# One step of attention in a slot, and weight norms taken from squares on ScalarE

## The chip, the core and the metric

The kernel runs on one core of a Trainium2 chip. TensorE (PE in the profile) multiplies, VectorE (DVE), ScalarE (ACT) and GpSimd (POOL) work on tiles, and SyncE (SP) starts most of the transfers. PSUM is the memory that TensorE writes its products into: here eight banks of 128 x 512 float32, three under the tag `acc` and five under the tag `w`. The metric is the device time of one launch in microseconds (us).

## What is computed

Attention with a window of 32 keys (in heads 4 to 7 every fourth key of the last 128), then a gated layer, then a second layer, on 4 x 576 = 2304 tokens of width 512:

```python
scores = scale * np.matmul(q, k.transpose(0, 1, 3, 2))        # 4 x 8 heads, 576 x 576, width 64
scores = np.where(masks[None, :, :, :], scores, -1000000000.0)
attn = softmax(scores)                                         # exp(s - max) / (sum + 1e-9)
x = (attn @ v), as 2304 x 512

xn = x / sqrt(mean(x * x) + 1e-6) * rms_g                      # the norm
g = xn @ w_gate;  val = xn @ w_val                             # 512 x 1536 each
y = (g * sigmoid(g) * val) @ w_out                             # 1536 x 512

h = y @ w_in                                                   # 512 x 2048
out = (max(h, 0) + alpha * min(h, 0)) @ w_out2                 # 2048 x 512
```

## The kernel before

**Products in three passes.** Each large operand is split into two float16 halves, high and low, and a product is three matmuls: high by high, high by low, low by high. Before it is split, a weight is scaled by a power of two. The scale of w_gate, w_val and w_out comes from a bound on the norms of their columns. The weights arrive as packed integers: `decode_w` turns them into float32 with three VectorE instructions for a block, or for a pair of blocks (lines 227, 228, 229). `norm_w` is called for each block after its decoding. For the 36 blocks of the first layer it forms, in bfloat16, the product of the block with itself on TensorE (`gram`, four 128 x 128 matmuls a block) and takes the row maximum on VectorE (line 281), up to four blocks to a reduction. The 12 columns of blocks come in two chunks, of 3 and of 9. When a chunk's last w_val block is in, `gram_w1` sends the maximum over the partitions (`over_partitions`, lines 335 and 338) through `root_scale` (lines 343 to 346); only then does `split_w` (lines 407 to 412) split that chunk's weights and the matmuls of `mm1` use them.

**Tokens and slots.** The tokens lie in seven blocks j of 256, 256, 384, 384, 384, 256 and 384 columns. Phase A of a block is the gated layer (`mm1`, 24 matmuls of a slot, then `mm2`, which sums into the `acc` tiles), phase B the second layer (`mm3`, 12 matmuls of a slot, then `mm4`). The order is A0, A1, A2, B0, B1, B2, A3, the first four slots of A4, B3, the rest of A4, A5, A6; the second layer of the last three blocks follows as a tail with fewer products (`mm3_t`, `mm4_t`, `out_t`), from about 813 us on. Each phase has 12 (A) or 16 (B) slots, one for each block of 128 columns of the layer's width.

**Attention between the slots.** Attention is cut into 52 groups of up to 128 queries. Groups 0 to 18 work in float32 (`f_` functions); the 33 groups from 19 on in float16 halves. Such a group takes two steps, and each step does one part of several groups at once: `first_half(i)` splits q and k of group i-1 into the tile `qkhl` (lines 538 to 552), computes the scores and softmax of group i-2 (`a_score`; it ends with `phl`, the probabilities in two halves, whose low half POOL makes on line 704), and issues two transposing transfers on SP: `qkT<-qkhl` (line 562) and `pT<-phl` (line 710). `second_half(i)` does the products with v of group i-3, the squares of group i and the next loads. A group's norm is a third kind of step. `qkhl` and `qkT` have one buffer each, so the scores of successive groups pass through one chain: split on ACT and DVE, transfer, eight score matmuls `psw<-qkT`, next split.

**What sets the order.** A planner at build time calls `take(d)` before each slot. It adds to a credit what the due times of the remaining steps ask for in that slot's time, and hands out steps, one for each unit of credit, up to two a slot. The steps run under a raised priority, and a scheduler then puts each engine's instructions into one fixed order. The weights are decoded by `pump`, called in the early slots.

Of the kernel before, what the change touches and what calls it, by code (L numbers as in the profile page):

```python
# [29 lines left out]
def kernel(  # L30
# [14 lines left out]
    nc = tc.nc  # L45
# [57 lines left out]
    def b_v(c):  # L103
        return 3 * c + 1

    def b_o(c):
        return 3 * c + 2
# [127 lines left out]
        d = dec_at[b]  # L235
        return wb[:, d * 512:(d + 1) * 512]

    def head(b):
        d = dec_at[b]
        return wbb[:, d * 1024:(d + 1) * 1024].rearrange("p (k f t) -> p k f t", f=128, t=2)[:, :, :, 1]  # L240

    def half(b, l):
        d = hl_at[b]
        return wb16[:, d * 1024 + l * 512:d * 1024 + (l + 1) * 512]
# [19 lines left out]
        ch = chunk(b // 3)  # L264
        return 2 * NCH + ch if b % 3 == 2 else 2 * ch + b % 3

    nrm = const.tile([128, 2, 3], F32, name="nrm")
    sqo = const.tile([128, NCH], F32, name="sqo")

    def gram(blocks, sums, dst):  # L270

        g = psw()
        last = len(blocks) - 1
        for n, b in enumerate(blocks):
            for kc in range(KD):
                w = head(b)[:, kc, :]
                if sums:
                    mm(g[:, 0:128], w, w, n + kc == 0, n == last and kc == KD - 1)
                else:
                    mm(g[:, n * 128:(n + 1) * 128], w, w, kc == 0, kc == KD - 1)  # L280
        nc.vector.tensor_reduce(dst, g[:, 0:128 if sums else (last + 1) * 128], axis=AX.X, op=ALU.max)

    def gram_w1(ch):
        cs = list(range(ch0[ch], ch0[ch + 1]))
        if len(cs) == 2:
            g = psw()
            for n, b in enumerate([f(c) for f in (b_g, b_v) for c in cs]):
                for kc in range(KD):
                    w = head(b)[:, kc, :]
                    mm(g[:, n * 128:(n + 1) * 128], w, w, kc == 0, kc == KD - 1)  # L290
            nc.vector.tensor_reduce(nrm[:, :, 0], g.rearrange("p (a c) -> p a c", a=2), axis=AX.X, op=ALU.max)
            parts = 1
        else:
            parts = (len(cs) + 3) // 4
            for a, f in enumerate((b_g, b_v)):
                for n in range(parts):
                    gram([f(c) for c in cs[4 * n:4 * n + 4]], False, nrm[:, a, n:n + 1])
        t = nrm[:, :, 0]
        if parts > 1:
            nc.vector.tensor_reduce(tmp2, nrm[:, :, 0:parts], axis=AX.X, op=ALU.max)  # L300
            t = tmp2
        over_partitions(t, 2, wp_[:, 0:2])
        two = slice(2 * ch, 2 * ch + 2)
        root_scale(wp_[:, 0:2], wsg[:, two], wrc[:, two])
        nc.vector.tensor_scalar(tsc[:, ch:ch + 1], xsc[:, 1:2], wrc[:, 2 * ch:2 * ch + 1], 0.5, ALU.mult, ALU.mult)

    def norm_w(b):
        if b < NW1:
            ch = chunk(b // 3)
            if b % 3 < 2:  # L310
                if b == b_v(ch0[ch + 1] - 1):
                    gram_w1(ch)
            elif b == b_o(ch0[ch + 1] - 1):
                gram([b_o(c) for c in range(ch0[ch], ch0[ch + 1])], True, sqo[:, ch:ch + 1])
        else:

            n, p = (b - NW1) // 2, (b - NW1) % 2
            junk = wk.tile([128, 512], BF16, tag="junk", bufs=1, name="junk")
            nc.scalar.activation(junk, dec(b), ACTF.Square, accum_out=sq2[:, p, n:n + 1])
            if b == NBLK - 1:  # L320
                g = psw()
                sb = const.tile([128, 2], F32, name="sb")
                nc.vector.tensor_reduce(sb, sq2, axis=AX.X, op=ALU.add)
                mm(g[:, 0:2], ones_1, eps[:, 0:2], True, False)
                mm(g[:, 0:2], ones_1, sb.bitcast(BF16).rearrange("p (n t) -> p n t", t=2)[:, :, 1], False, True)
                nc.vector.tensor_copy(sb2, g[:, 0:2])
# [791 lines left out]
    def out_t(t):  # L1118
# [50 lines left out]
    def take(d):  # L1169

        rate = max([(n - state["done"]) / max(when - state["clock"], 1.0) for n, when in need] + [0.0])
        state["credit"] = min(state["credit"] + rate * d, 4.0)
        got = []
        while steps and state["credit"] >= 1.0 and len(got) < 2:
            j = steps[0][1]
            if j is not None and j >= NXY and j - NXY not in done_b:
                break
            got.append(steps.popleft()[0])
            state["done"] += 1
            state["credit"] -= 1.0  # L1180
        return got
# [180 lines left out]
```

## Time and profile before

| | us |
|---|---|
| median of 3 runs (lowest, highest) | 984.36 (982.41, 986.07) |
| the profiled execution | 981.89 |
| its span | 980.0 |
| PE busy | 919.9 (94%) |
| DVE busy | 649.1 (66%) |
| ACT busy | 577.2 (59%) |
| POOL busy | 320.9 (33%) |
| SP's and other hardware queues' packets, share of 16 engines | 36.1% |
| granted TensorE clock, mean | 0.975 |

The span is what the profiler saw of the program, and the execution's time is 1.89 us longer. PE is busy for 94% of the span, so a change shows in the time mostly by what it does to the other 6%, to stretches in which PE's clock is lower, and to the first eighth of the span, where PE is not the busiest engine. "Idle before" in the rows below is the time in which an engine did nothing just before an instruction, with the engine and line whose result it then got.

### The profile page before, as it was taken

How to read it: one execution, taken by the hardware profiler on the slowest of the kernel's cores; microseconds unless marked ns; L12 is line 12 of the kernel's file. 1: busy time of each engine (PE TensorE's matmuls, PEld its weight loads, DVE VectorE, ACT ScalarE, POOL GpSimd, SP SyncE). 2: the span in 40 equal slices, each digit the busy share in tenths (PEclk: the TensorE clock that was granted, in tenths of full speed). 3: DMA queues.
4: the chain of work that ended last, by engine and by line, in shares of the span. 5: the costliest groups of instructions: out<-in, count | busy, mean ns of one | idle time of the engine just before them, and what ended most of it. 6: DMA issues, size and time to landing. Idle time of an engine off the chain costs nothing.

```text
span 980.0 us, 19290 instructions
## 1 busy us (share of the span) xinstructions
PE 919.9 (94%) x6958; PEld 628.0 (64%) x6958; DVE 649.1 (66%) x1586; ACT 577.2 (59%) x1600; POOL 320.9 (33%) x326
## 2 busy tenths in 40 slices
PE   5477899999999999999999989999999999999997
PEld 3466766775556666545555645555676557889986
DVE  4999997898898555554455565434454836776675
ACT  3434687676899876676655687644534325454553
POOL 2111631131354743332422233422352612332331
PEclk9777999999999999999999999999999999999999
DMA  9993436455445263452534564231311001000000
GB/s 254 315 354 98 116 99 187 119 182 147 91 85 96 58 121 65 92 103 61 117 64 83 98 111 87 53 82 29 52 27 22 1 1 33 1 23 2 23 23 22
DMA packets 191614, 88.15 MB, mean 90 GB/s; under 512 B 176800, under 2 KB 180384, under 8 KB 191520
## 3 DMA queue, kind: packets, MB, share of 16 engines
q1 hardware_dynamic: 189504, 83.27, 36.1%
q10 hardware_dynamic: 2016, 3.67, 1.1%
q8 instruction: 54, 0.88, 0.4%
q14 instruction: 40, 0.33, 0.1%
HBM read 55.32 MB, written 6.55 MB: 63 GB/s over the span
## 4 chain that ended last, share of the span: by engine, by line
PE 58%; DVE 3%; DMA 3%; ACT 2%; issue 2%; POOL 1%; SPq 0%; DVEq 0%; ACTq 0%; POOLq 0%
PE psw L95 25%; PE acc L95 17%; PE p L95 16%; DMA qkT<-qkhl 1%; DMA rkv<-in_k_dram 1%; DMA pT<-phl 1%; DVE wb L1049 0%; ACT wb L1048 0%; DMA xyall<-yhl 0%; ACT junk L512 0%; ACT s L589 0%; ACT qkhl L538 0%; ACT wb L407 0%; DVE s L1042 0%; DMA scratch<-xd 0%
## 5 line engine op out<-in xcount | busy, mean ns | idle before, releaser
L95 PEld LDWEIGHTS <-wb 128*128 128x128 f16 (+1 forms) x4917 | 458.3, 99 | 203.6 <-issue 11.8
L95 PE MATMUL psw<-xyall,wb 128*128 128x384 f16 (+1 forms) x2784 | 431.4, 304 | 2.7 <-DVE t L920 1.4
L95 PE MATMUL acc<-wb,hlall 128*128 128x512 f16 x771 | 187.7, 380 | 1.1 <-ACT hlall L923 0.6
L95 PEld LDWEIGHTS <-hlall 128*128 128x128 f16 x771 | 74.2, 98 | 74.5 <-ACT hlall L923 1.4
L929 POOL TENSOR_TENSOR hlall<-t,hlall 128x384 f16<-128x384 f32 (+1 forms) x56 | 53.8, 960 | 151.3 <-ACT hlall L923 126.8
L95 PE MATMUL acc<-wb 128*128 128x512 f16 x357 | 87.9, 384 | 3.2 <-ACT wb L987 1.9
L95 PE MATMUL p<-xyall,wb 128*128 128x256 f16 (+1 forms) x960 | 88.6, 251 | 0.0
L1097 POOL TENSOR_TENSOR wb<-fa,wb 128x640 f16<-128x640 f32 x32 | 47.0, 1472 | 108.5 <-ACT wb L1096 99.2
L95 PE MATMUL p<-wb 128*128 128x256 f16 x672 | 77.4, 273 | 0.0
L919 ACT ACTIVATE t<-psw,tsc 128x384 f32<-128x384 f32 (+1 forms) x84 | 44.2, 526 | 50.7 <-PE psw L95 50.5
L920 DVE SCALAR_TENSOR_TENSOR t<-t,psw 128x384 f32<-128x384 f32 (+1 forms) x84 | 41.0, 488 | 42.2 <-ACT t L919 42.0
L985 DVE SCALAR_TENSOR_TENSOR p<-m,nal,p 128x256 f32<-128x256 f32 (+1 forms) x64 | 42.9, 670 | 38.9 <-ACT p L984 37.8
L407 ACT ACTIVATE wb<-wb,wsg 128x512 f16<-128x512 f32 x68 | 46.0, 715 | 22.6 <-DVE wsg L345 15.6
L95 PE MATMUL psw<-wb 128*128 128x128 bf16 (+6 forms) x448 | 52.4, 284 | 6.4 <-DVE wb L229 6.4
L704 POOL TENSOR_TENSOR phl<-s,phl 96x512 f16<-96x512 f32 (+2 forms) x33 | 36.0, 1090 | 66.2 <-ACT phl L698 41.3
L589 ACT ACTIVATE s<-s,mx 96x128 f32<-96x128 f32 (+2 forms) x132 | 50.1, 384 | 11.4 <-DVE mx L581 11.3
L929 POOL TENSOR_TENSOR wb<-t,wb 128x256 f16<-128x256 f32 (+1 forms) x28 | 25.5, 911 | 95.3 <-ACT wb L923 84.0
L929 POOL TENSOR_TENSOR hlall<-p,hlall 128x256 f16<-128x256 f32 (+1 forms) x45 | 37.3, 829 | 51.9 <-ACT hlall L987 40.8
L921 DVE SCALAR_TENSOR_TENSOR t<-t,psw 128x384 f32<-128x384 f32 (+1 forms) x84 | 41.1, 490 | 18.4 <-PE psw L95 17.1
L1096 ACT ACTIVATE wb<-fa 128x640 f16<-128x640 f32 x32 | 23.6, 737 | 50.1 <-DVE fa L1089 50.1
L1095 DVE SCALAR_TENSOR_TENSOR wb<-fa,wb 128x384 f16<-128x384 f32 x32 | 40.9, 1286 | 18.0 <-ACT wb L1094 17.5
L410 POOL TENSOR_TENSOR wb<-wb 128x512 f16<-128x512 f32 x28 | 38.9, 1392 | 40.5 <-DVE wb L412 18.9
(197 smaller groups left out, 1403.2 us busy)
## 6 DMA issues: line engine op xcount, KB each, us to landing
wb<-in_moe_w_out_dram SPq DMA_DIRECT2D x28, 512.0 KB, 4.4
wb<-in_moe_w_in_dram SPq DMA_DIRECT2D x16, 512.0 KB, 3.8
wb<-in_moe_w_gate_dram SPq DMA_DIRECT2D x12, 512.0 KB, 7.0
wb<-in_moe_w_val_dram SPq DMA_DIRECT2D x12, 512.0 KB, 7.0
out_dram<-o ACTq DMA_DIRECT2D x14, 256.0 KB, 2.6
rkv<-in_k_dram SPq DMA_DIRECT2D x23, 128.0 KB, 2.7
rkv<-in_v_dram SPq DMA_DIRECT2D x23, 128.0 KB, 2.9
rq<-in_q_dram SPq DMA_DIRECT2D x23, 96.0 KB, 2.0
```

The source lines that it names most:

```text
L95: nc.tensor.matmul(o, a, b, start=start, stop=stop)
L407: nc.scalar.activation(half(b, 0), dec(b), ACTF.Copy, scale=wsg[:, s:s + 1])
L410: nc.gpsimd.tensor_tensor(half(b, 1), dec(b), half(b, 0), ALU.subtract)
L589: nc.scalar.activation(s[:nq, h, :nk], s[:nq, h, :nk], ACTF.Exp, bias=mx[:nq, 1, h:h + 1], accum_out=g["dn"][:nq, h])
L704: nc.gpsimd.tensor_tensor(phl[:nq, 1, :, :nk], g["s"][:nq, :, :nk], phl[:nq, 0, :, :nk], ALU.subtract)
L919: nc.scalar.activation(t[:, :T], pg[:, :T], ACTF.Tanh, scale=tsc[:, chunk(c):chunk(c) + 1])
L920: nc.vector.scalar_tensor_tensor(t[:, :T], t[:, :T], 1.0, pg[:, :T], ALU.add, ALU.mult)
L921: nc.vector.scalar_tensor_tensor(t[:, :T], t[:, :T], 2.0 ** -46, pv[:, :T], ALU.mult, ALU.mult)
L929: nc.gpsimd.tensor_tensor(a[:, 1, :T], t[:, :T], a[:, 0, :T], ALU.subtract)
L985: nc.vector.scalar_tensor_tensor(p[:, :T], m[:, :T], nal[:, c:c + 1], p[:, :T], ALU.mult, ALU.add)
L1095: nc.vector.scalar_tensor_tensor(l[:, 0:3], f[:, 0:3], 0.25, h[:, 0:3], ALU.mult, ALU.subtract)
L1097: nc.gpsimd.tensor_tensor(l[:, 3:8], f[:, 3:8], h[:, 3:8], ALU.subtract)
```

## The change

Three edits:

- **Norms.** `gram` and `gram_w1` go. `columns(b)` squares a block on ScalarE into one of four bfloat16 buffers (they lie in the third of the tiles that later hold the tokens' halves, `xyall`), and four matmuls, with 128 x 128 of the squares as the weights and one column of ones as the moving operand, write the column sums into a tile `cols` of PSUM, one column for each block. `cols` takes one of the three `acc` banks while the norms are formed. VectorE then reduces `cols` once a chunk (new line 289), and twice a chunk for w_out (new lines 296 and 297).
- **Last scaling.** For the last tile of the tail, the second half is scaled on VectorE in place, and its transfer starts from ACT's queue; the first half stays on ScalarE (line 1002).
- **Steps.** From the first of the steps of the float16 groups on, `take` hands out at most one step a slot; before it was two throughout.

```diff
+    cols = ps_a.tile([128, 512], F32, tag="acc", name="cols")[:, 0:6 * C1].rearrange("p (a c) -> p a c", c=C1)
+    sq_room = xyall[:, 2].rearrange("p a k t -> p (a k t)").bitcast(BF16)
+    sq_n = [0]
+
+    def columns(b):
+        n = sq_n[0] = (sq_n[0] + 1) % 4
+        junk = sq_room[:, n * 512:(n + 1) * 512]
+        nc.scalar.activation(junk, dec(b), ACTF.Square)
+        for kc in range(KD):
+            w = junk[:, kc * 128:(kc + 1) * 128]
+            if b % 3 < 2:
+                mm(cols[:, b % 3, b // 3:b // 3 + 1], w, ones_1[:, 0:1], kc == 0, kc == KD - 1)
+            else:
+                mm(cols[:, 2 + kc, b // 3:b // 3 + 1], w, ones_1[:, 0:1], True, True)
...
     def norm_w(b):
         if b < NW1:
             ch = chunk(b // 3)
-            if b % 3 < 2:
-                if b == b_v(ch0[ch + 1] - 1):
-                    gram_w1(ch)
+            cs = slice(ch0[ch], ch0[ch + 1])
+            columns(b)
+            if b == b_v(ch0[ch + 1] - 1):
+                nc.vector.tensor_reduce(tmp2, cols[:, 0:2, cs], axis=AX.X, op=ALU.max)
+                over_partitions(tmp2, 2, wp_[:, 0:2])
...
             elif b == b_o(ch0[ch + 1] - 1):
-                gram([b_o(c) for c in range(ch0[ch], ch0[ch + 1])], True, sqo[:, ch:ch + 1])
+                nc.vector.tensor_reduce(sq4, cols[:, 2:6, cs], axis=AX.X, op=ALU.add)
+                nc.vector.tensor_reduce(sqo[:, ch:ch + 1], sq4, axis=AX.X, op=ALU.max)
...
+    n_f32 = len(steps)
     for i in range(NFT, NG + 3):
         add(lambda i=i: first_half(i))
...
             i = 2 * t + n
+            if t == NT - 1 and n == 0:
+                nc.vector.tensor_scalar(yv[:, 0:512], yv[:, 0:512], rct[:, i:i + 1], None, ALU.mult)
...
+                nc.scalar.dma_start(out=out[r0:r0 + 128, :], in_=src)
+                continue
...
-        while steps and state["credit"] >= 1.0 and len(got) < 2:
+        while steps and state["credit"] >= 1.0 and len(got) < (2 if state["done"] < n_f32 else 1):
```

VectorE's order where the second chunk's scale is made, before. Here `wb` holds the weights, 1024 columns are a pair of blocks and 512 one block, `nrm` the maxima of the grams:

```order
L229 SCALAR_TENSOR_TENSOR wb<-wb 128x1024
L228 SCALAR_TENSOR_TENSOR wb<-wb 128x512
L227 TENSOR_SCALAR wb<-wb 128x512
L281 TENSOR_REDUCE nrm<-psw 128x1
L229 SCALAR_TENSOR_TENSOR wb<-wb 128x512
L228 SCALAR_TENSOR_TENSOR wb<-wb 128x512
L281 TENSOR_REDUCE nrm<-psw 128x1 x3
L229 SCALAR_TENSOR_TENSOR wb<-wb 128x512
L300 TENSOR_REDUCE tmp_103<-nrm 128x2
L335 TENSOR_SCALAR diag<-ident,tmp_103 128x128 x2
```

The same place after; `cols` are the column sums:

```order
L229 SCALAR_TENSOR_TENSOR wb<-wb 128x1024
L227 TENSOR_SCALAR wb<-wb 128x512
L228 SCALAR_TENSOR_TENSOR wb<-wb 128x512
L229 SCALAR_TENSOR_TENSOR wb<-wb 128x512
L227 TENSOR_SCALAR wb<-wb 128x512
L289 TENSOR_REDUCE tmp_104<-cols 128x2
L228 SCALAR_TENSOR_TENSOR wb<-wb 128x512
L318 TENSOR_SCALAR diag<-ident,tmp_104 128x128 x2
L229 SCALAR_TENSOR_TENSOR wb<-wb 128x512
```

From the pair's line 229 to the first `diag`, nine rows with five reductions of `nrm` and one of `tmp` have become seven with one reduction of `cols`, and one of the blocks' line 229 now stands behind `diag`.

POOL's order where phase A2 goes over into B0, before. A row `hlall<-t` or `hlall<-p` (line 929) stands for one slot (of phase A, of phase B), a row `phl<-s` (line 704) for the scores of one group; lines 410 split weights, line 737 is a norm:

```order
L410 TENSOR_TENSOR wb<-wb 128x512
L929 TENSOR_TENSOR hlall<-t,hlall 128x384
L410 TENSOR_TENSOR wb<-wb 128x512
L929 TENSOR_TENSOR hlall<-p,hlall 128x256 x2
L410 TENSOR_TENSOR wb<-wb 128x512
L704 TENSOR_TENSOR phl<-s,phl 96x512
L929 TENSOR_TENSOR hlall<-p,hlall 128x256
L410 TENSOR_TENSOR wb<-wb 128x512
L929 TENSOR_TENSOR hlall<-p,hlall 128x256
L737 TENSOR_TENSOR ms<-ms,mhalf 96x1
L929 TENSOR_TENSOR hlall<-p,hlall 128x256
L704 TENSOR_TENSOR phl<-s,phl 96x512
```

The same place after, from one group's scores earlier on (lines 913, 687, 393 and 720 are the old 929, 704, 410 and 737):

```order
L687 TENSOR_TENSOR phl<-s,phl 32x4x96
L393 TENSOR_TENSOR wb<-wb 128x512
L913 TENSOR_TENSOR hlall<-p,hlall 128x256 x2
L393 TENSOR_TENSOR wb<-wb 128x512
L687 TENSOR_TENSOR phl<-s,phl 96x512
L913 TENSOR_TENSOR hlall<-p,hlall 128x256 x2
L393 TENSOR_TENSOR wb<-wb 128x512
L913 TENSOR_TENSOR hlall<-p,hlall 128x256
L720 TENSOR_TENSOR ms<-ms,mhalf 96x1
L687 TENSOR_TENSOR phl<-s,phl 96x512
```

Before, the two groups whose scores these are come three slots of B0 apart. After, the first of them comes two slots behind the group ahead of it, still inside B0, and the second three.

POOL's order at the start of phase B3, before (`wb<-p` is also a slot of B, its halves kept in a weight's place; the memset on line 697 belongs to a group with fewer keys):

```order
L929 TENSOR_TENSOR hlall<-t,hlall 128x384
L697 MEMSET phl 32x8x32
L929 TENSOR_TENSOR hlall<-p,hlall 128x384
L929 TENSOR_TENSOR wb<-p,wb 128x384
L704 TENSOR_TENSOR phl<-s,phl 32x4x96
L929 TENSOR_TENSOR hlall<-p,hlall 128x384
L929 TENSOR_TENSOR wb<-p,wb 128x384
L704 TENSOR_TENSOR phl<-s,phl 96x512
L929 TENSOR_TENSOR hlall<-p,hlall 128x384
L929 TENSOR_TENSOR wb<-p,wb 128x384
L704 TENSOR_TENSOR phl<-s,phl 96x512
```

And after:

```order
L687 TENSOR_TENSOR phl<-s,phl 32x4x96
L913 TENSOR_TENSOR hlall<-p,hlall 128x384
L680 MEMSET phl 32x8x32
L913 TENSOR_TENSOR wb<-p,wb 128x384
L687 TENSOR_TENSOR phl<-s,phl 32x4x96
L913 TENSOR_TENSOR hlall<-p,hlall 128x384
L687 TENSOR_TENSOR phl<-s,phl 96x512
L913 TENSOR_TENSOR wb<-p,wb 128x384
L913 TENSOR_TENSOR hlall<-p,hlall 128x384
L687 TENSOR_TENSOR phl<-s,phl 96x512
L720 TENSOR_TENSOR ms<-ms,mhalf 96x1
L913 TENSOR_TENSOR wb<-p,wb 128x384
```

Before, the scores of the last three groups are two slots apart each. After, the same three (the second, third and fourth `phl` row) are one and two slots apart, and the first of them stands two slots behind the group ahead of it. The planner's rule, worked through for both versions, gives the numbers of steps: up to phase A2 they are alike; in A2 the new order falls one to two steps behind; then it takes one step in each of the slots 0 to 4 of B0 (before: one in each of 0, 2, 4, 6 and 8), one in each of 0 to 6 of B1 (before 2, 2, 1, 0, 1), and one in each of 0 to 12 of B3, which it enters two steps behind (122 against 124).

## Rows read from the trace of the kernel before

**Rows 1.** The page, busy time and share of PE, ACT and others.

```profile
PE 919.9 (94%) x6958; PEld 628.0 (64%) x6958; DVE 649.1 (66%) x1586; ACT 577.2 (59%) x1600; POOL 320.9 (33%) x326
```

**Rows 2.** Busy time by engine, 25 to 150 us in five stretches: their sum.

```profile
sum 125.00, PE 96.44 PEld 78.17 DVE 119.53 ACT 68.73 POOL 34.80; mean PE 19.29 PEld 15.63 DVE 23.91 ACT 13.75 POOL 6.96
```

**Rows 3.** Groups of instructions, 0 to 130 us: busy us, mean ns.

```profile
L95 PE MATMUL psw<-wb 128*128 128x128 bf16 x144 | 11.2, 239 | 6.4 <-DVE wb L229 6.4
...
L319 ACT ACTIVATE junk<-wb 128x512 bf16<-128x512 f32 x1 | 0.6, 620 | 0.0
```

**Rows 4.** VectorE's reductions of the grams: shortest, median, longest in ns.

```profile
L281 DVE TENSOR_REDUCE nrm<-psw x8: 282/614/682, 33.3 to 77.8; 128x1 f32<-128x512 f32 x4, 128x1 f32<-128x384 f32 x2, 128x1 f32<-128x128 f32 x2
...
L300 DVE TENSOR_REDUCE tmp<-nrm x1: 150/150/150, 79.0 to 79.0; 128x2 f32<-128x6 f32 x1
```

**Rows 5.** VectorE in time, 73 to 80 us: start, us, operation.

```profile
73.16 1.22 DVE L229 SCALAR_TENSOR_TENSOR wb<-wb 128x1024 int32<-128x1024 int32 x1
74.29 0.68 DVE L228 SCALAR_TENSOR_TENSOR wb<-wb 128x512 int32<-128x512 int32 x1
74.89 0.42 DVE L227 TENSOR_SCALAR wb<-wb 128x512 int32<-128x512 int32 x1
75.23 0.68 DVE L281 TENSOR_REDUCE nrm<-psw 128x1 f32<-128x512 f32 x1
75.83 0.68 DVE L229 SCALAR_TENSOR_TENSOR wb<-wb 128x512 int32<-128x512 int32 x1
...
77.03 1.48 DVE L281 TENSOR_REDUCE nrm<-psw 128x1 f32<-128x128 f32 x3
...
79.21 0.48 DVE L335 TENSOR_SCALAR diag<-ident,tmp 128x128 bf16<-128x128 f32 x2
```

**Rows 6.** PE in time, the grams and the second chunk's scale.

```profile
71.62 4.35 PE L95 MATMUL psw<-wb 128*128 128x128 bf16 x44 [3.26 <-DVE wb L229]
79.75 0.37 PE L95 MATMUL psw<-diag,ones 128*128 128x256 bf16 x1 [3.78 <-DVE diag L335]
...
118.22 2.23 PE L95 MATMUL psw<-wb 128*128 128x128 bf16 x36
```

**Rows 7.** What PE waited for from 120 to 800 us: sum, times, longest.

```profile
PE psw L95 <- DMA qkT<-qkhl: 4.5, 3, 2.2
...
PE psw L95 <- DMA pT<-phl: 1.6, 3, 0.9
```

**Rows 8.** PE in time, scores of five groups and the matmuls of slots.

```profile
300.69 0.63 PE L95 MATMUL psw<-qkT 128*96 128x128 f16 x8
...
312.15 0.65 PE L95 MATMUL psw<-qkT 128*96 128x128 f16 x8 [1.54 <-DMA qkT<-qkhl]
...
351.10 0.65 PE L95 MATMUL psw<-qkT 128*96 128x128 f16 x8 [2.23 <-DMA qkT<-qkhl]
...
499.16 2.10 PE L95 MATMUL acc<-wb,hlall 128*128 128x512 f16 x9
501.10 4.06 PE L95 MATMUL psw<-xyall,wb 128*128 128x384 f16 x24
505.00 2.11 PE L95 MATMUL acc<-wb,hlall 128*128 128x512 f16 x9
...
569.71 0.51 PE L95 MATMUL psw<-qkT 128*32 128x96 f16 x8 [0.69 <-DMA qkT<-qkhl]
...
578.15 0.61 PE L95 MATMUL psw<-qkT 128*96 128x128 f16 x8
```

**Rows 9.** Windows, after the longest wait: busy PE, PEld, DVE, ACT, POOL; clock; DMA.

```profile
352.00:355.00 3.00, 3.00 (x12) 1.48 (x11) 3.00 (x7) 2.14 (x7) 0.00 (x0) 0.50 0.41 90
```

**Rows 10.** The tile `qkhl`: its first split, and the transfer line 562.

```profile
L538 ACT ACTIVATE qkhl<-rq,sc x33: 703/722/747, 234.2 to 683.9; 96x512 f16<-96x512 f32 x23, 32x512 f16<-32x512 f32 x6, 64x512 f16<-64x512 f32 x4
...
DMA to landing us min/median/max: 3.3/3.8/5.0
```

**Rows 11.** The end: the last two scalings on ScalarE.

```profile
974.80 1.33 ACT L1002 ACTIVATE o<-yo,rct 128x512 f32<-128x512 f32 x2 [2.97 <-DVE yo L1128]
```

More of the change, by code (lines that the diff above doesn't have):

```diff
@@ L236, in dec @@
         return wb[:, d * 512:(d + 1) * 512]
-    def head(b):
-        d = dec_at[b]
-        return wbb[:, d * 1024:(d + 1) * 1024].rearrange("p (k f t) -> p k f t", f=128, t=2)[:, :, :, 1]
     def half(b, l):
@@ L265, in scale_of @@
         return 2 * NCH + ch if b % 3 == 2 else 2 * ch + b % 3
-    nrm = const.tile([128, 2, 3], F32, name="nrm")
     sqo = const.tile([128, NCH], F32, name="sqo")
[L270 to L305, printed above, removed]
+    sq4 = const.tile([128, KD], F32, name="sq4")
@@ L309, in norm_w @@
             ch = chunk(b // 3)
-            if b % 3 < 2:
-                if b == b_v(ch0[ch + 1] - 1):
-                    gram_w1(ch)
+            cs = slice(ch0[ch], ch0[ch + 1])
[3 more added lines that the diff above has]
+                over_partitions(tmp2, 2, wp_[:, 0:2])
+                two = slice(2 * ch, 2 * ch + 2)
+                root_scale(wp_[:, 0:2], wsg[:, two], wrc[:, two])
+                nc.vector.tensor_scalar(
+                    tsc[:, ch:ch + 1], xsc[:, 1:2], wrc[:, 2 * ch:2 * ch + 1], 0.5, ALU.mult, ALU.mult)
             elif b == b_o(ch0[ch + 1] - 1):
-                gram([b_o(c) for c in range(ch0[ch], ch0[ch + 1])], True, sqo[:, ch:ch + 1])
+                nc.vector.tensor_reduce(sq4, cols[:, 2:6, cs], axis=AX.X, op=ALU.add)
+                nc.vector.tensor_reduce(sqo[:, ch:ch + 1], sq4, axis=AX.X, op=ALU.max)
         else:
@@ L1132, in out_t @@
             i = 2 * t + n
+            if t == NT - 1 and n == 0:
+                nc.vector.tensor_scalar(yv[:, 0:512], yv[:, 0:512], rct[:, i:i + 1], None, ALU.mult)
+                (j, k), src = tiles[i], yv[:, 0:512]
+                assert blocks[j][0][0][1] >= (k + 1) * 128
+                r0 = blocks[j][0][0][0] + k * 128
+                nc.scalar.dma_start(out=out[r0:r0 + 128, :], in_=src)
+                continue
             o_tile(*tiles[i], yv[:, n * 512:(n + 1) * 512], rct[:, i:i + 1], nc.sync if n else nc.scalar)
```

## The prediction

> **What bounds the kernel now.** I read the page first: PE is busy for 94% of the span [rows 1], so DVE's, ACT's and POOL's totals decide nothing by themselves. Next came busy time by stretch. From 25 to 150 us DVE is busy for 119.5 of 125 us, PE for 96.4, ACT for 68.7 [rows 2]: there DVE sets the pace and ACT has 56 us to spare. After that PE sets it, except where it waits. The list of PE's waits from 120 to 800 us gives 4.5 us in three waits for `qkT<-qkhl` and 1.6 us in three for `pT<-phl` [rows 7]: 6.1 us that attention costs directly. The longest is 2.2 us, and in the stretch behind it, 352 to 355, PE's clock is 0.50 [rows 9], which is the level of 1.2 GHz against 2.4. Three us at half the level cost another 1.5 us. These two costs of attention, 7.6 us, and the DVE-bound start are what the change can reach; the rest is PE's own work.
>
> **The norms, DVE.** Out go the eight reductions of `nrm`: four of 0.68, two near 0.55 and two of 0.28 us by their forms, the two of `sqo` with the shape of the last (0.28), and line 300's 0.15 [rows 4], together 2.72 + 1.1 + 1.12 + 0.15 = 5.1 us. In come six small reductions, priced by line 300 at 0.15: 0.9. DVE loses 4.2 us of work in a stretch where it is 96% busy. What counts is the two chains up to the scales. For the second chunk the trace shows 73.16 to 79.21, 6.05 us, from the pair's line 229 to `diag` [rows 5]. The new order holds in that stretch one line 229 of 1024 columns (1.13, start to start), two lines 227 (0.34), three of the 0.60 us (228, 229, 228) and one small reduction (0.15) [rows 5]: 1.13 + 0.68 + 1.80 + 0.15 = 3.76. That is 2.3 us earlier. The reductions of the same chunk that stood further ahead give 0.8, the first chunk's two (0.55 and 0.55 against 0.15) 0.8: 3.9 us at best. PE stood idle for 3.26 us in front of the last grams and 3.78 us in front of `diag` [rows 6], so it can use this. One line 229 that came ahead of `diag` now comes behind it, 0.6 us that the splits of the weights meet later. I take -3.2 us, with ends -5 (all of DVE's 4.2 and some of PE's idle time) and +2 (below).
>
> **The norms, ACT and PE.** 36 squares, each 128 x 512 float32 to bfloat16; line 319 does just this in 0.62 us [rows 3], so 22.3 us on ACT, whose spare 56 us in that stretch [rows 2] cover them in sum. In order they are not free: ACT runs its queue as written, and a square that waits for DVE's line 229 holds back whatever stands behind it, the exponentials of the float32 groups among it; and the last square, its four matmuls and the reduction of `cols` are new links of the chain (0.62 on ACT, some 0.3 on PE). The +2 holds these links twice. On PE 144 matmuls of one column take the place of 144 of 128 columns, each with a 128-column load of weights ahead of it. In the trace 36 grams take 2.23 us, 62 ns a pair of load and matmul [rows 6], so all 144 cost 9 us where PE is idle for a quarter of the time; the new ones I take at the same 62, between 0 (the columns are what costs) and twice that. None of it reaches the end. `cols` holds one `acc` bank only until the first layer's weights are done; block 0, the only one that sums until then, needs two. The square's buffers lie in the third block's tile, which is written later.
>
> The Trainium skill ("TensorE: Matmul & The Clock Gate", section "LDWEIGHTS (loading the stationary operand)") has the load's time go by the stationary operand's columns, P / 1.2 ns: 107 ns for 128, whatever moves. By it the change spares PE nothing, and the 144 loads alone are an estimated 15 us, 6 more than the trace's 62 ns a pair give [rows 6], which disagrees with the size. If a third of these 6 came to lie on the path, the sum would be +4 in place of +2, by that rule.
>
> **One step a slot.** This moves no work in or out; it moves steps among slots, with their loads, their two transposing transfers on SP, and their POOL work. The question is how close the scores of two groups come on PE. One chain joins them, through the single buffers: split, transfer, scores. Its first split is 0.72 us and the transfer 3.3 to 5.0 us, median 3.8 [rows 10]; with the other three splits it needs about 6.2 us at the least. In the trace it shows more: the shortest pair among the close ones is 569.71 to 578.15, 8.4 us without a wait at its end, and 300.69 to 312.15 is 11.5 us with 1.54 of waiting [rows 8], under a loaded ACT and DVE. So PE needs at least about 8.5 us of other work between two scores, or it waits. How much stands there is counted from PE's order: a matmul of 384 columns is 162 ns (24 in 3.90 us, 501.10 to 505.00), of 512 columns 215 ns (9 in 1.94, 499.16 to 501.10) [rows 8], of 256 two thirds of the first.
>
> In the order before, pairs of steps in one slot leave 8.6 to 9.3 us at three places of A2 and of the change to B0, and 6.9 and 7.4 us in the change to B3; the waits of [rows 7] are there. In the new order A2 is even, 12.2 us between scores, and all waits there go. But the new order is behind, and makes up for it with one step in every slot: in B0 the score spacings are 6.4 and 7.2 us, in B1 7.1 (then 10.6), and in B3 7.3, 6.5, 8.8 and 4.4 us, the last where POOL's order has one slot between two groups. Against 8.5 these miss 2.1 + 1.3 + 1.4 + 1.2 + 2.0 + 4.1 = 12.1 us. What goes is the 4.5 of `qkT`, the longest of `pT`, 0.9 [rows 7], which lies in A2, and the 1.5 of the half clock: 6.9. The sum is +5.2. Its ends: -5 if the chain runs in its 6.2 us (then only 4.4 is too short, by 1.8), +13 if the 11.5 us of 300.69 to 312.15 hold in B0 and B1 too (worked out with the slower rival). I take the middle value because the 8.4 us row is the one with slots of B around it, as the new short places have.
>
> SP's order changes with the steps. Its transfers of a group stand one or two slots later in A2, where no product waits for them yet; the last norm of the fifth block falls one slot of A3 later and still lies a slot ahead of A4.
>
> **The tail.** The two scalings on ACT take 1.33 us together from 974.80 [rows 11]; with the second on DVE they can run side by side, up to 0.66 us earlier. But the transfer of the tile that ACT scales first goes out last to land and starts as before, so I take 0, with -0.5 to +0.2.
>
> **Sum.** -3.2 + 5.2 + 0 = +2.0 on the profiled execution of 981.89 us, which is its span of 980.0 and 1.9 around it: 983.9. That execution lies 2.5 us under the median, 984.36, of the runs shown; on the median it is 986.4, and I say 986. Own range of this case 981 to 990, a difference of 0.5% (4.9 us) either way being about what a measurement of this kernel can tell from none.
>
> **Rivals.**
> - *Slower: the chain stays at 11 us in B0 and B1.* Both phases have blocks of 256 columns, ACT and DVE there have the weights' splits too, and the one close pair in such surroundings took 11.5 us [rows 8]. From a spacing of 8.5 us on it decides. Four spacings there (6.4, 7.2, 7.1, 10.6) would miss 3.0, 3.0, 3.0 and 0.9 us more than I counted, 9.9; in the pair seen, 9.0 us of work in 11.5, 1.54 of the 2.5 missing showed as idle time, 0.62 of it, so 6.1, and one more stretch of half clock behind a wait over 2 us, 1.5 [rows 9]. 986 + 6.1 + 1.5 = 994. Against it: before, B0 was never asked for so much, so the 11.5 may be A2's own.
> - *Faster: even spacing is all that matters.* The three waits for `qkT` go (4.5 us) and the half clock with them (1.5), the 6.2 us chain fits into the close places of B0, B1 and B3 by work that is put ahead, and the start gives 3.2: 984.4 - 9.2 = 975. For it: 6.9 and 7.4 us of work in the change to B3 cost only 0.69 us for `qkT` [rows 8]. Against it: 4.4 us lies under any bound.
> - *The squares stand in the way.* ACT's queue order lets a waiting square hold up the exponentials, the start gains nothing and pays two squares (1.2 us): 986 + 3.2 + 1.2 = 990. Against it ACT's half-empty stretch [rows 2].
>
> **Chances.** My forecast 0.40, slower rival 0.25, faster 0.27, squares 0.08 (half of it over the bound). Faster 0.27, no difference 0.44, slower 0.29. The range that holds 8 in 10 reaches to both rivals, which have different signs: 974 to 995.
>
> **What would show it.** In the new trace: `diag` of the second chunk at about 76 instead of 79.2 us, the first matmuls of A0's second chunk as much earlier, and no wait for `cols` over 1 us; line 275 squares near 0.62 us; no wait for `qkT` between 295 and 352 us and no 0.50 clock there; then waits for `qkT<-qkhl` in B0, B1 and at B3's start of 8 to 12 us in sum. If these sum to under 5, the faster rival holds; over 17, the slower. I am wrong outright if PE's waits outside these places change by more than 3 us.

## The result, and the profile after

The changed kernel took 991.26 us, median of 6 runs (989.42 to 994.92), against 984.85 (982.41 to 986.32) before. The ratio is 1.0082, 95% interval 1.0061 to 1.0103: slower by 0.8%, more than the 0.5% that can be told from no change. The forecast was 986, the range 974 to 995. The time lies inside the range, 5 us above the forecast and 3 below the slower rival's 994; "no difference", which had the largest chance, did not come.

The profiled execution took 990.53 us. Its page, the line that answers to [rows 1], then the sum from 25 to 150 us that answers to [rows 2]:

```profile
PE 916.1 (93%) x6958; PEld 623.5 (63%) x6958; DVE 644.3 (65%) x1582; ACT 596.3 (60%) x1635; POOL 322.9 (33%) x326
```

```profile
sum 125.00, PE 95.58 PEld 74.85 DVE 116.30 ACT 89.24 POOL 36.08; mean PE 19.12 PEld 14.97 DVE 23.26 ACT 17.85 POOL 7.22
```

DVE lost 3.2 us in this stretch and ACT gained 20.5; 4.2 and 22.3 were reckoned for the whole kernel, where the page has 4.8 and 19.1. The groups that answer to [rows 3, 4], with what each waited for behind the last bar:

```profile
L275 ACT ACTIVATE xyall<-wb 128x512 bf16<-128x512 f32 x36 | 21.4, 630 | 22.6 <-DVE wb L229 17.1 <-DMA wb<-in_moe_w_gate_dram 2.3 <-DVE dn L579 1.4
...
L95 PE MATMUL cols<-ones,xyall 128*128 128x1 bf16 x144 | 8.3, 167 | 20.0 <-ACT xyall L275 20.0
...
L289 DVE TENSOR_REDUCE tmp<-cols 128x2 f32<-128x18 f32 x1 | 0.2, 170 | 0.0
```

The squares take 630 ns, the small reduction 0.17 us. DVE's and PE's way to the second chunk's scale, in order of time, answers to [rows 5, 6]:

```profile
67.91 1.23 DVE L229 SCALAR_TENSOR_TENSOR wb<-wb 128x1024 int32<-128x1024 int32 x1
...
71.17 0.17 DVE L289 TENSOR_REDUCE tmp<-cols 128x2 f32<-128x18 f32 x1
...
71.90 0.47 DVE L318 TENSOR_SCALAR diag<-ident,tmp 128x128 bf16<-128x128 f32 x2
```

```profile
60.52 0.53 PE L95 MATMUL cols<-ones,xyall 128*128 128x1 bf16 x15
...
69.85 0.27 PE L95 MATMUL cols<-ones,xyall 128*128 128x1 bf16 x4 [7.56 <-ACT xyall L275]
...
72.43 0.37 PE L95 MATMUL psw<-diag,ones 128*128 128x256 bf16 x1 [1.58 <-DVE diag L318]
```

`diag` stands at 71.9 us where it stood at 79.2. This is not the luck of one profile: in the ten profiles with the new norms (the runs below are counted in) it stands between 71.9 and 77.6 us, in the four with the old between 79.2 and 81.1. PE's 7.56 us in front of a column sum are its wait for a square that waits for decoding; it stands where the waits of 3.26 and 3.78 us stood. PE's waits from 120 to 800 us answer to [rows 7]:

```profile
PE psw L95 <- DMA qkT<-qkhl: 9.3, 7, 3.0
PE acc L95 <- ACT hlall L907: 6.9, 5, 2.8
...
PE acc L95 <- POOL hlall L913: 2.3, 3, 1.0
PE acc L95 <- ACT hlall L971: 2.2, 2, 1.8
...
PE psw L95 <- DMA pT<-phl: 1.0, 2, 0.8
```

The waits for `qkT` have doubled. Waits for `hlall` (the halves that one slot's end hands to the products that sum it up) now come to 11.4 us in sum. Before they came to 1.1, of which the longest was:

```profile
PE acc L95 <- ACT hlall L923: 0.6, 1, 0.6
```

The scores that answer to [rows 8], in the change to B0 and at the start of B3:

```profile
300.51 0.52 PE L95 MATMUL psw<-qkT 128*32 128x96 f16 x8 [0.56 <-DMA qkT<-qkhl]
...
311.39 0.65 PE L95 MATMUL psw<-qkT 128*96 128x128 f16 x8 [2.99 <-DMA qkT<-qkhl]
...
320.54 0.65 PE L95 MATMUL psw<-qkT 128*96 128x128 f16 x8 [1.12 <-DMA qkT<-qkhl]
```

```profile
572.59 0.52 PE L95 MATMUL psw<-qkT 128*32 128x96 f16 x8 [1.35 <-DMA qkT<-qkhl]
...
589.39 0.61 PE L95 MATMUL psw<-qkT 128*96 128x128 f16 x8
...
594.93 0.65 PE L95 MATMUL psw<-qkT 128*96 128x128 f16 x8 [0.53 <-DMA qkT<-qkhl]
```

In B3 scores follow each other after 5.5 us with a wait of 0.53.

To compare two profiles stretch by stretch I add up PE's products (columns over 2.4 GHz, four times that for float32, grams and column sums left out; the sum is the same in every kernel here, some 880 us) and take the time at which the same sum is reached. The table gives that time minus the time in the first profile of before, at points named by the latter's time. Its runs are told of below; "cap" is the edit that hands out one step a slot.

| us, against before's first profile | 171 | 207 | 227 | 249 | 331 | 470 | 629 | 744 | 888 |
|---|---|---|---|---|---|---|---|---|---|
| before, second profile (e10) | +4.0 | +4.0 | +4.0 | +3.8 | +4.4 | +5.1 | +4.5 | +4.6 | +4.5 |
| cap alone (e2) | +2.7 | +2.7 | +2.7 | +2.4 | +10.4 | +7.8 | +10.9 | +13.9 | +13.9 |
| the changed kernel | -4.9 | -5.3 | -2.6 | -0.9 | +5.7 | +3.3 | +5.1 | +9.2 | +9.3 |
| norms alone (e1) | +0.5 | +0.2 | +4.8 | +5.0 | +6.9 | +7.4 | +7.8 | +8.1 | +8.1 |
| norms, last scaling (e3) | -1.4 | -1.8 | +3.2 | +3.2 | +6.2 | +7.2 | +8.0 | +8.3 | +8.3 |
| e3, A1's end mended (e4) | -4.4 | -4.8 | -5.7 | -5.9 | +0.7 | -0.8 | 0.0 | 0.0 | 0.0 |
| e4 with the cap (e6) | -2.7 | -3.1 | -4.0 | -4.9 | +3.5 | +1.1 | +3.4 | +7.7 | +7.7 |
| e6, subtraction on GpSimd (e9) | -4.0 | -4.3 | -5.2 | -5.8 | +2.2 | +0.2 | +3.1 | +3.6 | +3.7 |
| e4, fewer splits on ACT (e11) | -2.4 | -2.7 | -3.6 | -4.5 | -1.6 | -5.0 | -5.6 | -5.6 | -5.6 |

Two profiles of one kernel differ by 4 us up to 171 us, so a single profile says little of the start; and the first profile of before was a short one (981.89 us, the second 986.42). Of the others those of e1 and e3 were long (989.97 and 989.57, medians 987.54 and 986.03) and that of e11 short (975.56, median 979.84). What a version is worth is therefore taken from the ratios below, and the table shows the places.

### The profile page after: what moved, and what is told of

The parts are those of the page before. It is cut to its first block, busy times and chain, and to the rows that moved or that the text cites. A ratio compares the mean times of both kernels' runs of the same rounds, so it can differ in the third digit from the quotient of the medians.

```text
span 988.6 us, 19323 instructions
## 1 busy us (share of the span) xinstructions
PE 916.1 (93%) x6958; PEld 623.5 (63%) x6958; DVE 644.3 (65%) x1582; ACT 596.3 (60%) x1635; POOL 322.9 (33%) x326
## 4 chain that ended last, share of the span: by engine, by line
PE 60%; DVE 13%; DMA 8%; ACT 8%; issue 5%; SPq 3%; POOL 1%; POOLq 0%; ACTq 0%; DVEq 0%
PE psw L95 26%; PE acc L95 17%; PE p L95 16%; DVE wb L228 2%; DMA qkT<-qkhl 2%; DVE wb L229 2%; DVE wb L227 1%; ACT wb L390 1%; ACT s L572 1%; DMA rkv<-in_k_dram 1%; DMA wb<-in_q_dram 1%; SPq L608 1%; SPq L208 1%; ACT junk L495 1%; DVE wb L395 1%
## 5 line engine op out<-in xcount | busy, mean ns | idle before, releaser
L95 PEld LDWEIGHTS <-wb 128*128 128x128 f16 x4773 | 447.0, 98 | 193.2 <-issue 6.2
L95 PE MATMUL acc<-wb,hlall 128*128 128x512 f16 x771 | 190.6, 382 | 11.6 <-ACT hlall L907 6.9
L907 ACT ACTIVATE hlall<-t 128x384 f16<-128x384 f32 (+1 forms) x56 | 26.9, 480 | 42.0 <-DVE t L905 41.9
L393 POOL TENSOR_TENSOR wb<-wb 128x512 f16<-128x512 f32 x28 | 36.9, 1320 | 41.5 <-ACT wb L392 22.6
```

The source lines that it names most:

```text
L393: nc.gpsimd.tensor_tensor(half(b, 1), dec(b), half(b, 0), ALU.subtract)
```

## The experiments

The ratios are to the kernel before in the same job, with 95% intervals.

**e1, norms alone; e2, cap alone; e3, all but the cap.** Each takes its part of the diff over unchanged, as

```diff
-        while steps and state["credit"] >= 1.0 and len(got) < (2 if state["done"] < n_f32 else 1):
+        while steps and state["credit"] >= 1.0 and len(got) < 2:
```

for e3, and for e1 also without the last scaling's seven lines.

> The kernel before with the norms edit alone (two steps a slot, both last scalings on ScalarE). In the changed kernel the same PE work is reached 5.0 us earlier than before at 171 us, and 4.4 us of this are lost again between 207 and 249 us. Theory 1 (the loss belongs to the capped order of steps): here the lead of about 5 us stays past 250 us, and the time is 4 to 5 us under before, ratio 0.995 to 0.996. Theory 2 (the loss belongs to the earlier start itself: in A1 and A2 the second layer's weights come no faster, and an ACT queue with their squares waits for them): the lead is gone by 250 us here too, and the time is 0 to 1 us under before, ratio 0.999 to 1.000.

> The kernel before with one step a slot alone (grams on PE, both last scalings on ScalarE). Theory 1: the capped order costs what the changed kernel lost against before between 207 and 629 us (10.4 us at equal PE work, of which the waits for qkT are 9.3 against 4.5) and the 4.2 us at 735 us where DVE was held up beside POOL, so +10 to +15 us, ratio 1.010 to 1.015; waits of PE for qkT over 8 us in sum. Theory 2: 4.4 of the 10.4 us are not the cap's, so +6 to +10 us, ratio 1.006 to 1.010. If the 4.2 us at 735 us are an accident of timing, they are missing here and either is 4 us less.

> The changed kernel with two steps a slot again: norms and last scaling changed, the order of steps as before. In the changed kernel the end comes 0.6 to 0.7 us better against before than the last stretch of PE work does, which the last scaling on two engines may be worth. Both theories expect 0.5 to 0.7 us less than the norms alone; so theory 1 a ratio of 0.994 to 0.996 to before, theory 2 of 0.998 to 1.000. The 735 us stretch has no wait of PE over 1 us if its 4.2 us come from the capped order.

Measured: e1 1.0014 (0.9992 to 1.0035), e2 1.0117 (1.0082 to 1.0153), e3 1.0019 (1.0000 to 1.0039). The cap is what makes the kernel slower, and the norms bring nothing by themselves. Neither theory holds whole: e2 has the ratio of theory 1, and e1 and e3 lie a little above those of theory 2. But for the loss at 207 to 249 us theory 2 holds, since it is in both kernels without the cap, 4.6 to 5.0 us between 207 and 227, and not in the cap alone. The place in e1, DVE and then PE in order of time:

```profile
213.01 0.41 DVE L904 SCALAR_TENSOR_TENSOR t<-t,psw 128x256 f32<-128x256 f32 x1
213.34 0.68 DVE L228 SCALAR_TENSOR_TENSOR wb<-wb 128x512 int32<-128x512 int32 x1
213.95 0.41 DVE L227 TENSOR_SCALAR wb<-wb 128x512 int32<-128x512 int32 x1
214.28 0.14 DVE L719 TENSOR_SCALAR ms<-ms 96x1 f32<-96x1 f32 x1
214.34 1.27 DVE L229 SCALAR_TENSOR_TENSOR wb<-wb 128x512 int32<-128x512 int32 x2
215.55 0.40 DVE L905 SCALAR_TENSOR_TENSOR t<-t,psw 128x256 f32<-128x256 f32 x1
```

```profile
216.46 1.31 PE L95 MATMUL acc<-wb,hlall 128*128 128x512 f16 x4 [2.37 <-ACT hlall L907]
```

The two instructions that close a slot of `mm1`, lines 904 and 905, are 2.5 us apart, with five rows between them of which four decode weights of the second layer. The slot is the tenth of A1's twelve; before, its two instructions are 1.0 us apart. Behind them ACT makes `hlall`, and PE, which has reached that slot's `mm2`, waits 2.37 us (2.38 in e3 and in the changed kernel). Before, PE's one wait over 0.5 us from 122 to 240 us is for something else, and no half clock follows it:

```profile
216.58 0.55 PE L750 MATMUL psw<-ident,wb 96*128 96x96 f32 x4 [1.53 <-DVE wb L738]
```

In e1 PE then runs at half clock for a while; the windows from 200 to 250 us of before and of e1 (the third number from the end is the clock):

```profile
200.00:250.00 50.00, 47.77 (x331) 30.92 (x330) 45.34 (x114) 32.55 (x95) 12.63 (x11) 1.00 0.61 169
```

```profile
200.00:250.00 50.00, 46.07 (x300) 29.57 (x300) 43.13 (x105) 31.31 (x93) 11.37 (x10) 0.93 0.58 157
```

1.00 against 0.93 of 50 us is 3.5 us; with the longer wait this is the loss. So theory 2 had the right edit but not the cause in its words: it is not the weights' arrival but where the new order puts their decoding.

**e4, no decoding in the last slot of A1**, on e3:

```diff
-            state["pump"] = state.get("pump", 0.0) + PUMP[j]
+            state["pump"] = state.get("pump", 0.0) + (0.0 if (j, c) == (1, 11) else PUMP[j])
```

> Norms and last scaling changed, two steps a slot, and in addition no weight block is decoded in the last slot of A1 (it is decoded from A2 on). In the runs with the norms changed and two steps a slot, PE waits 2.4 us at the end of A1 for a half of hlall, because VectorE's order has about 2.2 us of decoding between the two instructions that close one slot, and then runs some us at the half clock: 4.6 us are lost there against before. Theory (the norms' gain at the start is lost by this order): the wait and the half clock at 207 to 227 us go, and the time is 3 to 5 us under the norms with the last scaling, ratio to before 0.997 to 0.999. Rival (the stretch is limited by the arrival of the second layer's weights): the wait moves into A2 and the ratio stays at 1.001 to 1.003.

Measured: 0.9974 (0.9955 to 0.9994), faster than both kernels. The wait and the stretch in e4:

```profile
209.69 1.04 PE L95 MATMUL acc<-wb,hlall 128*128 128x512 f16 x4 [0.58 <-ACT hlall L907]
```

```profile
200.00:250.00 50.00, 48.37 (x330) 30.05 (x328) 43.26 (x100) 32.04 (x98) 9.75 (x11) 1.00 0.57 152
```

The pair of the tenth slot is 1.6 us apart. The wait is 0.58 us in place of 2.37, the clock stays at 1.00, and the lead that the start gives is still 5.9 us at 249 us.

**e5, the subtraction at 735 us on GpSimd**, on the changed kernel:

```diff
-        nc.vector.tensor_tensor(s[:, 1], x12, x11, ALU.subtract)
+        nc.gpsimd.tensor_tensor(s[:, 1], x12, x11, ALU.subtract)
```

> The changed kernel whole, with the first subtraction of each remade weight (x12 - x11) on GpSimd in place of VectorE. In the changed kernel and in the cap alone this subtraction takes 3.58 us on VectorE at 732 us beside four additions on GpSimd that run back to back; before and in both kernels with two steps a slot it takes 1.36. Theory (the 4.2 us lost at 735 us are this instruction held up beside GpSimd): the wait of PE for hlall at 735 us, 2.8 us, and the half clock behind it go, and the time is 3 to 4 us under the changed kernel, ratio to before 1.004 to 1.006. Rival (the order of the slot's closing instructions behind it is what costs, whatever stands ahead): the wait stays over 1.5 us and the ratio at 1.007 to 1.009.

First the place in the changed kernel, on POOL, DVE and PE. The remaking of the last layer's weights has begun; DVE's first subtraction starts beside the second of four additions on POOL and ends 0.3 us after the last of them:

```profile
730.79 0.66 POOL L913 TENSOR_TENSOR wb<-t,wb 128x256 f16<-128x256 f32 x1
731.42 1.15 POOL L1023 TENSOR_TENSOR f<-wb 128x512 f32<-128x512 f16 x1
732.53 1.15 POOL L1024 TENSOR_TENSOR f<-wb 128x512 f32<-128x512 f16 x1
...
734.75 1.14 POOL L1024 TENSOR_TENSOR f<-wb 128x512 f32<-128x512 f16 x1
```

```profile
732.60 3.58 DVE L1026 TENSOR_TENSOR s<-f 128x256 f32<-128x256 f32 x1 [2.94 <-POOL f L1023]
736.10 0.41 DVE L904 SCALAR_TENSOR_TENSOR t<-t,psw 128x256 f32<-128x256 f32 x1
736.54 0.42 DVE L905 SCALAR_TENSOR_TENSOR t<-t,psw 128x256 f32<-128x256 f32 x1
```

```profile
737.47 1.89 PE L95 MATMUL acc<-wb,hlall 128*128 128x512 f16 x4 [2.80 <-ACT hlall L907]
```

Lines 904 and 905, queued behind it, close a slot some 3 us late; PE waits 2.80. In e3 the subtraction takes 1.36 us:

```profile
736.35 1.36 DVE L1026 TENSOR_TENSOR s<-f 128x256 f32<-128x256 f32 x1 [1.15 <-POOL f L1023]
```

In POOL's order of all kernels with a cap the low half of a slot (line 913) comes after the norm's last row (738) and directly ahead of the additions; without one it is the other way round, and the additions begin 0.08 us after it. Why this lets DVE in between the additions or not, no run shows. Measured for e5: 1.0059 (1.0040 to 1.0078) against 1.0082, whose intervals overlap, and some 0.5 us lost here in place of 4.2. DVE in e5:

```profile
736.20 0.42 DVE L905 SCALAR_TENSOR_TENSOR t<-t,psw 128x256 f32<-128x256 f32 x1
738.42 3.79 DVE L1028 TENSOR_TENSOR s<-f 128x256 f32<-128x256 f32 x1 [1.80 <-POOL f L1024]
```

```profile
744.05 1.04 PE L95 MATMUL acc<-wb,hlall 128*128 128x512 f16 x4 [0.37 <-ACT hlall L907]
```

DVE is held up as long as before, 3.79 us, now at another subtraction; but the slot's closing rows come ahead of it, and PE waits 0.37. So theory was right in the gain and wrong in its reason: the rival's reason, what is queued behind, decides. (e9 below makes the same edit to e6; there the intervals stand apart.)

**e6, e4 with the cap; e7 and e8, the cap for a part of the steps** (as e6, `done` counts steps; e7 caps from the 112th on, e8 up to it):

```diff
-        while steps and state["credit"] >= 1.0 and len(got) < 2:
+        while steps and state["credit"] >= 1.0 and len(got) < (2 if state["done"] < 112 else 1):
```

> The changed kernel whole, with no weight block decoded in the last slot of A1. Without the cap this kernel had a ratio of 0.997 to before. Theory (the cap costs 8 to 12 us by itself: waits for hlall in A2, for qkT in B0, B1 and B3, and the held-up subtraction at 735 us; the end of A1 is the norms' affair): ratio 1.006 to 1.009, the 2.4 us wait at 208 us gone. Rival (with the late wait of A1 gone the capped order meets its due times in A2 and loses no more than the 4 us at 735): ratio 1.000 to 1.003.

> As the kernel with norms, last scaling and no decoding in the last slot of A1, and one step a slot only from the 112th step on, so from the end of B2 to the end. Theory: 1.8 us more in B3 and 4.2 us more at 735 us than without any cap, ratio to before 1.002 to 1.005; PE waits about 2.8 us for hlall near 730 us; no loss against the uncapped kernel before 550 us. Rival (the close scores in B3, 4.4 us of work apart, cost what was predicted, 7 us): ratio 1.008 or more.

> The same with one step a slot from the first float16 group up to the 112th step, two after it. Theory: the loss of A2, B0 and B1, 5 to 8 us by 400 us, and the 4.2 us at 735 us, since GpSimd's order there is that of the capped kernel too: ratio to before 1.006 to 1.009. If the loss of A2 to B1 is not the cap's, 1.002 to 1.004.

Measured: e6 1.0053 (1.0036 to 1.0069), e7 1.0048 (1.0033 to 1.0064), e8 1.0022 (1.0000 to 1.0043). Against e4's 0.9974 the cap costs 0.8%, some 8 us. By the table most of it lies late. From 227 to 470 us e6 loses 5.1 us and e4, without a cap, 4.9. From 470 to 629 us e6 loses 2.3 and e4 0.8; the step to 744 us costs 4.3 and nothing. e7 and e8 both pay the latter (about 3 us each). e7 came out as its theory had it, e6 a little under its own. e8 missed its theory and has the ratio given for the other case, that A2 to B1 cost nothing by the cap: they cost less than I had thought after e2.

**e9, e6 with e5's edit; e10, before once more**, for a second profile.

> The changed kernel whole, with no weight block decoded in the last slot of A1 and with the first subtraction of each remade weight on GpSimd, so with both costs taken away that the runs have found: 4.6 us at the end of A1 (the norms' order) and 4.2 us at 735 us (the capped order beside GpSimd). Theory (little of the cap's cost is left after these two, 1 to 3 us in B3): ratio to before 0.999 to 1.002. Rival (the close scores in B0, B1 and B3 hold the larger part, as predicted): 1.004 or more.

> The kernel before, profiled once more, since its one profile (981.89 us) lies 2 to 3 us under the median of its runs, and every comparison at equal PE work leans on it. Between its two profiles there should be differences of 1 to 3 us in the first 150 us and of 1 to 3 us between 250 and 470 us, both from stretches of half clock; what the changed kernel loses beyond these is the change's.

Measured: e9 1.0017 (1.0001 to 1.0032), as theory had it. It still lies 4.2 us above e4, 0.9974; the profiles put some 2 of them between 470 and 629 us, and for the rest no run names a place. e10's one profile took 986.42 us; it differs from the first by 4.0 us before 171 us, more than I had expected and not by the clock, whose mean up to there is 0.89 in both, and by 1.1 from 207 to 470. e2, the cap on the old start, loses 5.1 there; so in these profiles the cap costs about 4 us in A2 to B1 without the norms, and with them nothing that shows.

**e11, fewer splits on ScalarE, on e4; e12, the same on before.** A low half that ScalarE begins is finished by a subtraction on GpSimd; the others are made on VectorE alone. So the edit takes work off both ScalarE and GpSimd:

```diff
-    LO1, LO2 = 3, 2
+    LO1, LO2 = 3, 4
```

> The best version so far (norms and last scaling changed, two steps a slot, no decoding in the last slot of A1), with every fourth in place of every second of the second layer's weights scaled once more on ScalarE for its low half; the others take VectorE. That is 8 instructions of 0.71 us off ScalarE and 8 of 0.66 us onto VectorE between 250 and 310 us. Theory (the lead of 5 us from the start runs into a stretch, 260 to 320 us, in which ScalarE is busy for 19 to 20 of every 20 us, and is given back there): ScalarE's stretch gets 5 us shorter, the lead at 331 us is kept to 3 us or more where it was lost (+0.7), ratio to before 0.993 to 0.996. Rival (the lead is lost to the attention's chain of transfers and scores): ratio 0.996 to 0.999, as without this edit.

> The kernel before with that edit alone. Theory: without a lead to keep, ScalarE's fullness costs little there, ratio 0.998 to 1.000. If the edit is worth the same with and without the norms, 0.996 or less, the stretch bound the kernel before as well.

The kernels that come to 249 us ahead of before fall back by 470 us, capped or not: e4 by 5.1 us, e6 by 6.0, the changed kernel by 4.2 (before's own second profile by 1.3). Busy time from 260 to 320 us, the sum of three windows, for before, e4 and e11:

```profile
sum 60.00, PE 57.23 PEld 35.87 DVE 52.51 ACT 57.89 POOL 29.66; mean PE 19.08 PEld 11.96 DVE 17.50 ACT 19.30 POOL 9.89
```

```profile
sum 60.00, PE 55.54 PEld 34.47 DVE 46.30 ACT 56.90 POOL 26.33; mean PE 18.51 PEld 11.49 DVE 15.43 ACT 18.96 POOL 8.78
```

```profile
sum 60.00, PE 57.50 PEld 35.42 DVE 54.04 ACT 58.26 POOL 24.62; mean PE 19.17 PEld 11.81 DVE 18.01 ACT 19.42 POOL 8.21
```

ACT is busy for 57 to 58 of 60 us in all of them. Measured: e11 0.9946 (0.9925 to 0.9967), e12 1.0003 (0.9987 to 1.0019). e11 is the fastest version here, 979.84 us, and the same edit without the norms is worth nothing; the one ratio lies within the theory's range, the other at its end. In e11's profile, the shortest of its six runs, the lead is 4.5 us at 249 us and 5.0 at 470, but 1.6 at 331, where theory had 3 or more.

The theory's cause is argued and not shown. The step from e4 to e11, 0.0028, is not clear of the two intervals. ACT is as full in e11 as in e4. And from 220 to 340 us six subtractions of 1.18 us have left GpSimd as well (line 393, 14 in e4 and 8 in e11), which no run tells apart. What the profiles do show is the last window, 300 to 320 us, in e4 and in e11:

```profile
300.00:320.00 20.00, 16.42 (x128) 11.07 (x126) 15.87 (x48) 19.30 (x60) 7.66 (x8) 0.91 0.47 93
```

```profile
300.00:320.00 20.00, 18.03 (x151) 12.46 (x149) 17.57 (x53) 19.69 (x62) 8.23 (x8) 1.00 0.52 104
```

At 310 us PE waits for `qkT` in both, 2.38 us in e4 and 1.74 in e11, and only in e4 the clock falls to half behind it, 0.91 in the mean of this window. From 249 to 470 us e4's clock costs it some 3 us (0.98 of 82 us and 0.99 of 139; 1.00 and 1.00 in e11) of the 5.6 by which the two differ there. So the rival, the attention's chain of transfers and scores, may have a part in it.

## Why the prediction came out as it did

- **The start, -3.2 us: right, somewhat small.** At 171 us the ten profiles with the new norms stand between -4.9 and +0.5, mean -2.8; the four with the old (0, +0.4, +2.7, +4.0) have a mean of +1.8. The gain is about 4.5 us, beside a spread of 4 to 5 within either kind. The chain from the pair's line 229 to `diag` was reckoned at 3.76 and is 3.99 (67.91 to 71.90). "No wait for `cols` over 1 us" was wrong: VectorE waits 1.6 us for them at line 296, and PE 7.56 for the squares that they are summed from.
- **The step that failed: the sum took the -3.2 of the start through to the end.** I took the norms edit as done with at 150 us. Its new order moved the second layer's decoding between the closing rows of A1's tenth slot: 4.6 us, three quarters of it clock (e1, e4). And with that mended the lead is gone again by 470 us, in a stretch in which ScalarE is full (e4); that this is why is argued and not shown (e11). As they stand, the norms are worth nothing, as e1 shows, and not 3.2 us.
- **One step a slot, +5.2 us: the sign right, the size small, the place mostly wrong.** By ratio the cap costs 6.2 us on e3, 7.8 on e4 and 11.5 on before. The waits for `qkT` sum to 9.3 us where 12.1 were counted, and at the places named, B0, B1 and B3's start, to 7.4, a little under the 8 to 12 given. In B0 and B1 the three that I counted at 2.1 + 1.3 + 1.4 = 4.8 us are 2.99 + 1.12 + 1.41 = 5.5, though the spacings there, 9.1 to 10.9 us, are longer than my floor of 8.5. In B3 that floor, taken from the 8.4 us row, was too high: there scores come 5.5 us apart, under even the 6.2 us worked out from the chain's own rows, and three misses priced at 7.3 us show 1.9 of waits. In A2, even as it is, PE waits 1.34 us for `qkT` at 247 us and 0.56 at 301; before it had none there to lose, since the waits at 312 and 351 us lie in B0. The half clock at 352 us went, as foretold. But "no wait for `qkT` between 295 and 352 us" could not hold beside short spacings in B0, which lies there.
- **By its own sign the prediction was wrong outright.** It said so for the case that PE's waits outside the named places change by more than 3 us. The waits for `hlall`, of which it has no word, went from 1.1 to 11.4 us. The longest are at 211 us (2.38, the norms' order), 373 us (1.83) and 737 us (2.80, the next item); three near 1 us are in A2. That the time still fell into the range is in part luck: too much was counted in B3, and nothing for these waits, and the two errors partly cancel.
- **A cost I did not have:** 4.2 us at 735 us, long after the last close score. The order row that goes with it in every kernel with a cap, a norm's last row one place earlier on POOL, is in the changed order; I compared the orders around scores only. By e5 and e9 what costs is that the slot's closing rows stand behind the held-up subtraction.
- **The tail, 0: 0.6 us are gained, just past the end of -0.5.** From the last matmul's start to the span's end it is 6.87 to 6.91 us in the five profiles without the edit, and 6.28 to 6.30 in eight of the nine with it (6.61 in e9). The prediction had the right transfer: the one that lands last is the second of the tile that ACT scales first, and it starts 1.26 us after that scaling began, in the kernel before and in the changed one. But it does not land as long after that: 2.98 us before, 2.36 after. Starts before, then after, in order of time, and the medians from issue to landing:

```profile
975.55 1.11 SPq L1007 DMA_DIRECT2D out_dram<-o  x2
976.16 0.36 ACTq L1007 DMA_DIRECT2D out_dram<-o  x1
```

```profile
984.06 0.72 ACT L986 ACTIVATE o<-yo,rct 128x512 f32<-128x512 f32 x1 [2.97 <-DVE yo L1112]
984.45 0.34 ACTq L1122 DMA_DIRECT2D out_dram<-yo  x1
984.80 1.11 SPq L991 DMA_DIRECT2D out_dram<-o  x2
```

```profile
out_dram<-o SPq DMA_DIRECT2D x2, 128.0 KB, 2.8
```

```profile
out_dram<-o SPq DMA_DIRECT2D x2, 128.0 KB, 2.3
```

  The other tile's transfer now starts ahead of it and no longer beside it; that this is why it lands sooner is not shown.
- **The sum.** -3.2 + 5.2 + 0 stood for +2 us. The runs give by ratio, in steps of 985 us: norms with the last scaling +1.9 (e3), all three +8.1; with A1's end mended -2.6 (e4) and, with the cap, +5.2 (e6), of which 3.5 go with the subtraction (e9). The slower rival, 994, had nearly the right time for a wrong reason: it wanted 7.6 us more in B0 and B1 than was counted there, and they hold 0.7 more.

What stays open: why the cap costs about 4 us in A2 to B1 on the old start and next to nothing on the new one, beyond that both meet the full ScalarE; where the rest of the cap's cost lies that e9 still has; what of the lead ScalarE takes by 470 us, and what the waits for `qkT` with their half clock; and what decides whether GpSimd's additions let VectorE in.

## What to carry to other kernels

An edit that frees an engine also re-deals the order of everything that a scheduler places after it. So after pricing the edit, look through the whole new order for rows that came between the two instructions which close a slot, or for closing rows that now stand behind a row that can be held up; here two such places, one from the norms and one from the cap, both far from the edits, cost 8.8 us, where the start had gained some 4.5. And a lead at the start need not reach the end: follow it through the later stretches in which an engine is full or PE waits, and try to widen these together with the edit (here 8 splits moved to VectorE went with a step from 0.9974 to 0.9946, whose intervals overlap).

## What the hardware showed that was not expected

- A subtraction of 128 x 256 on VectorE, 0.41 us alone, took 3.58 us beside the last three of four back-to-back additions on GpSimd (3.79 in e5, beside two of them and what GpSimd did next), and 1.36 beside the same additions in e3.
- A load of 128 columns with a matmul of one column, back to back, costs PE far less than the 62 ns of a gram: the 15 at 60.52 us stand for 0.53 us, 35 ns each with the last one's end in it. The 107 ns a load of the Trainium skill ("TensorE: Matmul & The Clock Gate", section "LDWEIGHTS (loading the stationary operand)") would make it an estimated 1.6 us; the trace disagrees, and the change did spare PE. One such load by itself has a mean record of 103 ns, near that figure; in the row above loads follow each other after 25 ns, so they overlap.
- Runs of one kernel spread over 8 to 9 us: the 23 of before beside e1 to e3 went from 980.25 to 988.18 and its two profiles are 4 us apart by 171 us.
